# Two places of a block turn: VectorE's order and SyncE's queue where attention hands over to token mixing

## The chip, the cores and the metric

The kernel runs on one core of one Trainium2 chip. The metric is the time of one execution on the device, in microseconds (us); the number that counts is the median of several runs. The engines are named as the profile names them: PE (TensorE, matmuls), DVE (VectorE), ACT (ScalarE), POOL (GpSimd) and SP (SyncE, which here only issues transfers).

## The reference

Two stages follow each other. The first is attention restricted to clusters, for 4 batches, 8 heads, 768 tokens and 64 channels a head: each query and key is assigned to the nearest of 16 centroids, and a query sees only the keys of its own cluster. The second takes the result as `x` (4 x 768 x 512) and mixes tokens:

```python
theta = x @ w_theta
cos_t, sin_t = (np.cos(theta), np.sin(theta))
zr = x * cos_t
zi = x * sin_t
yr = np.einsum('ts,bsd->btd', w_tok_r, zr)
yi = np.einsum('ts,bsd->btd', w_tok_i, zi)
y = yr + yi
u = x + y
return (u + np.maximum(u @ w_ch, 0.0)).astype(np.float32)
```

`w_theta` is drawn large enough that the angle `theta` goes over many periods, so it is wrapped to one period before the sine.

## The kernel before, in words

Attention works through 16 pairs of heads, each in 12 units (two halves of the queries by six tiles of keys). Per unit TensorE makes the row maxima ahead of time and the scores (L374), ScalarE the exponentials (L437), GpSimd the sums of the exponentials (L448), and TensorE the weighted values (L509). What has to happen beside the units (assigning clusters, loading and splitting weights, normalising) is cut into pieces, and tables of unit numbers say at which unit each piece is recorded (`stages`, `at_unit`). `in_order` then ties the instructions of each engine to the order in which they were recorded, as far as the units go; behind that, in the mixing stage, a scheduler sets the order on each engine.

The normalised output of a pair goes to DRAM (`xT_d`, L533), with channels on partitions. The reciprocal of the row sums takes four small transfers on SyncE's queue: the sums out (`sd<-se`, L489), back in another layout (`sq<-sd`, L492), after the reciprocal on VectorE (L494) out again (`sd<-sq`, L495), and in, broadcast (`rb<-sd`, L499). VectorE or GpSimd multiplies by `rb` (L530).

Mixing goes through the 24 token tiles (4 batches of 6 tiles of 128 tokens). For each tile:

- `rotation_parts`: `x` is split in a high and a low part (`xh` on ScalarE, L581; `xl` on VectorE, L583).
- `rotation_turn`: `x` is needed a second time with tokens on partitions. Four transfers bring it from DRAM in blocks of 32 x 32 (`xb`, L596, in `load_blocks`), and one instruction on VectorE turns the blocks (`xn<-xb`, L601). `xb` has one buffer, so the blocks of the next tile are loaded when this turn has been done; `rotation_turn` issues these loads itself.
- `rotation_angle`: twelve matmuls make the angle in PSUM (`tp`, L608).
- `rotation_reduce`: VectorE wraps it to one period (`kk`, L613; `r`, L614 and L615) and ScalarE takes the absolute value (`ab`, L617).
- `rotate`: sine and cosine on ScalarE (L823), the products with `xn` on VectorE (L825), high and low parts on ScalarE (L828) and GpSimd (L830).

Then `mix` multiplies by the token weights (L876), and after the sixth tile `channel` does the last product (L899). The angle of a tile is recorded two tiles ahead of its mixing (`AHEAD`).

The change lies where the stages meet. Tile 0 is rotated while attention still runs: `first_rotation` is a generator in five pieces, recorded at units `NUT - 10 + (0, 3.5, 4, 6, 7)`. Each `yield` ends a piece:

```python
FIRST = (0, 3.5, 4, 6, 7)
stages([NUT - 10 + k for k in FIRST], first_rotation())
```

All later tiles go through `theta`, in the mixing stage; the scheduler is free to set their instructions between those of the last units. Tile 1's angle lies in the PSUM bank that tile 0's had. Beside this the last of the weight chunks is prepared: VectorE's L137 to L146 make a chunk, SyncE writes it out (`wd5i<-w`, L156). In the mixing stage SyncE reads such chunks back (`kept`, L789).

Of the kernel before, what the change touches and what calls it, by code (L numbers as in the profile page):

```python
# [41 lines left out]
def kernel(  # L42
# [153 lines left out]
    def m_tile(name):  # L196
        return ps0.tile([P, 2, 512], F32, tag="m", name=name)
# [352 lines left out]
    def first_rotation():  # L550

        xs = ma[0].tile([P, NCT, P], F32, tag="ab", name="xs")
        nc.sync.dma_start(out=xs, in_=xT_d[0][:, :, 0:P])
        yield
        load_blocks(0)
        xh, xl, xn, kk, r = rotation_tiles(0, "0_0")
        rotation_parts(xs, xh, xl)
        yield
        tp = m_tile("tp0_0")[:, 0]
        rotation_turn(0, xn)  # L560
        yield
        rotation_angle(xh, xl, tp)
        yield
        ab = rotation_reduce(0, "0_0", tp, kk, r)
        first.update(r=r, ab=ab, xn=xn)

    first = {}

    def rotation_tiles(n, name):
        pool = ma[n % 2]  # L570
        xh = pool.tile([P, NCT, P], F32R, tag="xh", name=f"xh{name}")
        xl = pool.tile([P, NCT, P], F32R, tag="xl", name=f"xl{name}")
        xn = pool.tile([P, DM], F32, tag="xn", name=f"xn{name}")
        kk = ma[0].tile([P, DM], I32, tag="kk", name=f"kk{name}")
        return xh, xl, xn, kk, pool.tile([P, DM], F32, tag="r", name=f"r{name}")

    def behind(x):
        return tc.issue_after(x.ins) if x is not None else nullcontext()

    def rotation_parts(xs, xh, xl, after=None):  # L580
        nc.scalar.copy(out=xh, in_=xs)  # L581
        with behind(after):
            nc.vector.tensor_tensor(out=xl, in0=xs, in1=f(xh), op=ALU.subtract)  # L583
# [3 lines left out]
    def load_blocks(n):  # L587
        if n == B * NT:
            return
        b, t = divmod(n, NT)  # L590
        xb = blocks[n] = ma[0].tile([P, DM], F32, tag="xb", name=f"xb{n}")


        for a in range(P // 32):
            src = xT_d[b][:, :, t * P + 32 * a:t * P + 32 * a + 32]
            nc.sync.dma_start(  # L596
                out=xb[32 * a:32 * a + 32].rearrange("c (n m r) -> c n m r", n=NP, m=P // 32),
                in_=src.rearrange("(m c) n r -> c n m r", c=32))

    def rotation_turn(n, xn):  # L600
        nc.vector.transpose(out=xn, in_=blocks.pop(n))  # L601
        load_blocks(n + 1)

    def rotation_angle(xh, xl, tp):
        n = 0
        for xx, k in ((xh, 0), (xh, 1), (xl, 0)):
            for c in range(NCT):
                nc.tensor.matmul(tp, lhsT=xx[:, c, :], rhs=w_th[c][k], start=(n == 0), stop=(n == 3 * NCT - 1))  # L608
                n += 1

    def rotation_reduce(n, name, tp, kk, r):

        nc.vector.tensor_scalar_mul(kk, tp, INV_2PI)  # L613
        nc.vector.scalar_tensor_tensor(out=r, in0=kk, scalar=-C1, in1=tp, op0=ALU.mult, op1=ALU.add)  # L614
        nc.vector.scalar_tensor_tensor(out=r, in0=kk, scalar=-C2, in1=r, op0=ALU.mult, op1=ALU.add)  # L615
        ab = ma[n % 2].tile([P, DM], F32, tag="ab", name=f"ab{name}")
        nc.scalar.activation(out=ab, in_=r, func=AF.Abs)  # L617
        return ab
# [76 lines left out]
    for x, gen in enumerate(early_weights()):  # L695
        stages(W_FIRST if x == 0 else [W_EVERY * (x - 1) + k for k in W_UNITS], gen)

    stages([NUT - 10 + k for k in FIRST], first_rotation())


# [52 lines left out]
    def mbank(name):  # L753
        return pm.tile([P, 512], F32, tag="bank", name=name)
# [49 lines left out]
    def theta(b, t):  # L804
        n, name = b * NT + t, f"{b}_{t}"
        xs = xts[b][:, :, t * P:(t + 1) * P]
        xh, xl, xn, kk, r = rotation_tiles(n, name)

        late = n == AHEAD
        rotation_parts(xs, xh, xl, last_out[0] if late else None)  # L810
        rotation_turn(n, xn)
        tp = mbank(f"tp{name}")
        with behind(last_rows[0] if late else None):
            rotation_angle(xh, xl, tp)
        ab = rotation_reduce(n, name, tp, kk, r)
        rotate(b, t, r, ab, xn)

    def rotate(b, t, r, ab, xn):
        z = []
        for nm_, tr, sc_, bi_ in (("c", ab, -1.0, halfpi), ("s", r, 1.0, 0.0)):  # L820

            with tc.issue_after(before_sin[0].ins):
                nc.scalar.activation(out=tr, in_=tr, func=AF.Sin, scale=sc_, bias=bi_)  # L823
            with tc.issue_after(before_mul[0].ins):
                nc.vector.tensor_tensor(out=tr, in0=tr, in1=xn, op=ALU.mult)  # L825
            zh = mz.tile([P, DM], F32R, tag="zh" + nm_, name=f"zh{nm_}{b}_{t}")
            zl = mz.tile([P, DM], F32R, tag="zl" + nm_, name=f"zl{nm_}{b}_{t}")
            split = nc.scalar.copy(out=zh, in_=tr)  # L828
            with tc.issue_after(last_acc[0].ins):
                nc.gpsimd.tensor_tensor(out=zl, in0=tr, in1=zh.bitcast(F32), op=ALU.subtract)  # L830
            z.append((zh, zl))
        if (b, t) == (0, 0):

            before_sin[0], before_mul[0] = split, last_sum[0]
        zs[b, t] = z
# [95 lines left out]
    for n in range(1, AHEAD):  # L931
        theta(*order[n])
    late_weights = late()
    for n, (b, t) in enumerate(order):
        if n + AHEAD < len(order):
            nb, nt = order[n + AHEAD]
            if nt == 0:
                load_x(nb)
            theta(nb, nt)
        if b == 0:  # L940
            next(late_weights, None)
        if b < B - 1 or t < NT - TAIL:
            mix(b, t)
            if t == NT - 1:
                channel(b)
# [61 lines left out]
```

## Time and profile before

| what | us |
|---|---|
| median of 3 runs | 795.83 |
| lowest and highest | 795.07 and 797.3 |
| the profiled execution's own time | 797.01 |
| its span, first to last instruction | 795.2 |
| TensorE busy | 774.7 (97%) |
| VectorE busy | 573.3 (72%) |
| GpSimd busy | 488.4 (61%) |
| ScalarE busy | 386.9 (49%) |
| mean granted TensorE clock | 0.991 |

Times in the views are counted from the start of the span. A row of the timeline gives start, duration, engine, line, operation, what it writes and reads, and in brackets how long the engine had stood idle ahead of it and what ended that. `SPq` is SyncE's queue: such a row is the issue of a transfer, not the transfer. A row of the windows gives the window, its length, the busy time of PE, PEld (weight loads), DVE, ACT and POOL with the number of instructions, the granted clock, the share of the transfer engines' time, and GB/s.

### The profile page before, as it was taken

To read this page: it belongs to the slowest core of one execution; us is meant where nothing else is said; L and a number is where in the kernel's file an instruction comes from. 1 tells how busy PE (TensorE), PEld (TensorE's weight loads), DVE (VectorE), ACT (ScalarE), POOL (GpSimd) and SP (SyncE) were. 2 spreads that over 40 slices of the span, in tenths; PEclk is the share of its full clock that TensorE was granted. 3 is DMA by queue.
4 is the path that set the end of the run, shared out by engine and by line. 5 is a ranking of instruction groups with operands and counts; after the bars stand their busy time and mean duration, and the time that the engine had idled before them with its cause. 6 is when DMAs were issued, how large, how long until landed. Compare 5 with 4: busy or idle time off the path is not lost.

```text
span 795.2 us, 14306 instructions
## 1 busy us (share of the span) xinstructions
PE 774.7 (97%) x5538; PEld 574.3 (72%) x5538; DVE 573.3 (72%) x688; ACT 386.9 (49%) x777; POOL 488.4 (61%) x284
## 2 busy tenths in 40 slices
PE   7999999999999999999999599999999999999998
PEld 5665656565665666666665378899888988899998
DVE  5889999999999999999889368954435343634322
ACT  3466666666767676666655335451324123403310
POOL 3479888999999999888988141571125122332131
PEclk9999999999999999999999899999999999999999
DMA  3233314342443234433352267024111411030001
GB/s 120 61 96 97 110 55 148 124 115 73 143 132 112 85 127 152 131 108 125 123 187 69 68 177 237 17 41 166 20 27 28 158 28 27 14 93 14 1 21 61
DMA packets 81584, 73.45 MB, mean 92 GB/s; under 512 B 59588, under 2 KB 65324, under 8 KB 81132
## 3 DMA queue, kind: packets, MB, share of 16 engines
q1 hardware_dynamic: 81228, 72.10, 30.5%
q8 instruction: 44, 0.72, 0.4%
q10 hardware_dynamic: 288, 0.43, 0.1%
q14 instruction: 24, 0.20, 0.1%
HBM read 57.08 MB, written 15.32 MB: 91 GB/s over the span
## 4 chain that ended last, share of the span: by engine, by line
PE 92%; DVE 5%; DMA 1%; SPq 1%; issue 1%; ACT 1%; DVEq 0%; ACTq 0%
PE y L876 26%; PE sc L374 25%; PE av L509 16%; PE tp L608 8%; PE cy L899 5%; PE m L374 3%; PE cp L899 3%; PE sm L476 2%; PE lg L263 1%; PE y L899 1%; DVE nm L396 1%; PE lt L275 1%; PE mt L404 1%; DVE acc L452 1%; SPq L596 1%
## 5 line engine op out<-in xcount | busy, mean ns | idle before, releaser
L437 ACT ACTIVATE at<-sc 128x384 f32<-128x384 f32 x384 | 173.6, 494 | 96.7 <-PE m L374 57.7
L396 DVE TENSOR_REDUCE nm<-m 128x1 f32<-128x768 f32 x192 | 179.7, 945 | 19.6 <-PE m L374 16.6
L448 POOL TENSOR_TENSOR acc<-at,at 128x768 f32<-128x768 f32 x64 | 130.4, 2038 | 40.0 <-ACT at L437 40.0
L374 PE MATMUL m<-hk,hq 64*128 64x384 f32 x384 | 147.2, 388 | 0.9 <-DVE nm L396 0.8
L509 PE MATMUL av<-at,vt 128*64 128x384 f32 x768 | 145.7, 499 | 1.4 <-ACT at L437 1.1
L448 POOL TENSOR_TENSOR acc<-acc,at 128x768 f32<-128x768 f32 x64 | 131.7, 2059 | 10.1 <-ACT at L437 8.0
L830 POOL TENSOR_TENSOR zlc<-ab,zhc 128x512 fp32r<-128x512 f32 x24 | 32.1, 1336 | 172.1 <-ACT zhc L828 172.1
L374 PE MATMUL m<-mk,mq 64*128 64x384 f32 x384 | 127.7, 336 | 0.6 <-DVE mk L303 0.6
L374 PE MATMUL sc<-hq,hk 64*128 64x384 f32 x384 | 117.0, 389 | 0.5 <-ACT at L437 0.5
L374 PEld LDWEIGHTS sc<-hq,hk 64*128 64x128 f32 x384 | 55.8, 183 | 61.9 <-issue 27.8
L374 PE MATMUL sc<-lq,hk 64*128 64x384 f32 x384 | 97.6, 335 | 0.0
L374 PE MATMUL sc<-mq,mk 64*128 64x384 f32 x384 | 97.4, 334 | 0.0
L374 PE MATMUL sc<-hq,lk 64*128 64x384 f32 x384 | 97.2, 333 | 0.0
L509 PEld LDWEIGHTS av<-at,vt 128*64 128x64 f32 x768 | 46.7, 136 | 60.5 <-issue 53.6
L613 DVE TENSOR_SCALAR kk<-tp 128x512 int32<-128x512 f32 x24 | 16.4, 683 | 79.4 <-PE tp L608 79.4
L374 PEld LDWEIGHTS m<-hk,hq 64*128 64x128 f32 x384 | 70.6, 185 | 3.5 <-DVE nm L396 2.7
L374 PEld LDWEIGHTS m<-mk,mq 64*128 64x128 f32 x384 | 71.3, 187 | 1.0 <-ACT hq L356 1.0
L452 DVE TENSOR_TENSOR acc<-acc,acc 128x768 f32<-128x768 f32 x30 | 70.7, 2357 | 0.0
L581 ACT CAST xh<-xT 128x512 fp32r<-128x512 f32 x23 | 14.3, 622 | 99.8 <-PE tp L608 99.8
L890 POOL TENSOR_TENSOR ul<-xT,uh 128x384 fp32r<-128x384 f32 (+1 forms) x36 | 33.5, 955 | 35.5 <-ACT uh L889 34.9
L374 PEld LDWEIGHTS sc<-lq,hk 64*128 64x128 f32 x384 | 54.9, 185 | 0.0
L374 PEld LDWEIGHTS sc<-mq,mk 64*128 64x128 f32 x384 | 54.9, 184 | 0.0
(160 smaller groups left out, 1713.3 us busy)
## 6 DMA issues: line engine op xcount, KB each, us to landing
rawq<-in_qT_dram SPq DMA_DIRECT2D x16, 384.0 KB
vt<-in_v_dram SPq DMA_DIRECT2D x16, 384.0 KB
rb<-sd SPq DMA_DIRECT2D x32, 192.0 KB
xT_d<-xt SPq DMA_DIRECT2D x16, 384.0 KB
xb<-xT_d SPq DMA_DIRECT2D x96, 64.0 KB
rawk<-in_kT_dram SPq DMA_DIRECT2D x15, 384.0 KB
w<-in_wrT_dram SPq DMA_DIRECT2D x6, 768.0 KB
w<-in_wiT_dram SPq DMA_DIRECT2D x6, 768.0 KB
```

Source lines behind the costliest of these rows:

```text
L374: nc.tensor.matmul(out, lhsT=stat[r, cols], rhs=mov[r, over], start=start, stop=stop)
L396: nc.vector.tensor_reduce(out=s["nm", a][:, j, i // 2:i // 2 + 1], in_=s["m", j][:, :, 0:HS], op=ALU.max, axis=AX.XY, negate=True)
L437: last_exp[0] = nc.scalar.activation(out=s["at", a, i][:, j], in_=s["sc", j], func=AF.Exp, scale=SCALE)
L448: last_acc[0] = nc.gpsimd.tensor_tensor(out=s["acc", a, x], in0=prev, in1=at, op=ALU.add)
L452: nc.vector.tensor_tensor(out=s["acc", a, 0], in0=s["acc", a, 0], in1=s["acc", a, 1], op=ALU.add)
L509: nc.tensor.matmul(s["av"][64 * j:64 * j + 64], lhsT=s["vt"][:, i, j, :], rhs=s["at", a, i][:, j], start=(i == 0), stop=(i == NT - 1))
L608: nc.tensor.matmul(tp, lhsT=xx[:, c, :], rhs=w_th[c][k], start=(n == 0), stop=(n == 3 * NCT - 1))
L613: nc.vector.tensor_scalar_mul(kk, tp, INV_2PI)
L830: nc.gpsimd.tensor_tensor(out=zl, in0=tr, in1=zh.bitcast(F32), op=ALU.subtract)
L876: nc.tensor.matmul(y_at(b, d, c0, c1), lhsT=zz[:, d * P:(d + 1) * P], rhs=ww[:, c0:c1], start=first and lead, stop=last, skip_group_check= ...
L890: nc.gpsimd.tensor_tensor(out=ul[:, d, :], in0=x, in1=uh[:, d, :].bitcast(F32), op=ALU.subtract)
L899: nc.tensor.matmul(cp, lhsT=w_c[d][k][:, e * P:(e + 1) * P], rhs=uu[:, d, :], start=(n == 0), stop=(n == 3 * NCT - 1), skip_group_check=True)
```

## The change

In `first_rotation` the load of tile 0's blocks moves into the first piece, next to the load of the tile itself. The turn of a tile's blocks, with the loads of the next tile's blocks that it issues, moves from ahead of the angle to behind its wrapping, in `first_rotation` and in `theta`.

```diff
         nc.sync.dma_start(out=xs, in_=xT_d[0][:, :, 0:P])
-        yield
         load_blocks(0)
+        yield
         xh, xl, xn, kk, r = rotation_tiles(0, "0_0")
         rotation_parts(xs, xh, xl)
         yield
         tp = m_tile("tp0_0")[:, 0]
+        yield
+        rotation_angle(xh, xl, tp)
+        yield
+        ab = rotation_reduce(0, "0_0", tp, kk, r)
         rotation_turn(0, xn)
-        yield
-        rotation_angle(xh, xl, tp)
-        yield
-        ab = rotation_reduce(0, "0_0", tp, kk, r)
         first.update(r=r, ab=ab, xn=xn)
...
         rotation_parts(xs, xh, xl, last_out[0] if late else None)
-        rotation_turn(n, xn)
         tp = mbank(f"tp{name}")
         with behind(last_rows[0] if late else None):
             rotation_angle(xh, xl, tp)
         ab = rotation_reduce(n, name, tp, kk, r)
+        rotation_turn(n, xn)
         rotate(b, t, r, ab, xn)
```

VectorE's order at the handover, before. `xn_0` and `xn_1` are the turns of tiles 0 and 1, `kk` and `r` the wrappings, `sq` the reciprocal of a pair's sums, `ab_0` tile 0's first product:

```order
L146 SCALAR_TENSOR_TENSOR w_5615<-w_5614,w_5615 128x768
L601 STREAM_TRANSPOSE xn_0_5829<-xb_5822 128x512
L601 STREAM_TRANSPOSE xn_1_6062<-xb_5846 128x512
L494 RECIPROCAL sq_5886<-sq_5886 128x12
L613 TENSOR_SCALAR kk_0_5830<-tp_0_5844 128x512
L614 SCALAR_TENSOR_TENSOR r_0_5831<-kk_0_5830,tp_0_5844 128x512
L615 SCALAR_TENSOR_TENSOR r_0_5831<-kk_0_5830,r_0_5831 128x512
L613 TENSOR_SCALAR kk_1_6063<-tp_1_6073 128x512
L583 TENSOR_TENSOR xl_3_6209<-xT_6021,xh_3_6208 128x512
L614 SCALAR_TENSOR_TENSOR r_1_6064<-kk_1_6063,tp_1_6073 128x512
L615 SCALAR_TENSOR_TENSOR r_1_6064<-kk_1_6063,r_1_6064 128x512
L825 TENSOR_TENSOR ab_0_5918<-ab_0_5918,xn_0_5829 128x512
```

The same place with the change:

```order
L146 SCALAR_TENSOR_TENSOR w_5615<-w_5614,w_5615 128x768
L494 RECIPROCAL sq_5880<-sq_5880 128x12
L613 TENSOR_SCALAR kk_0_5830<-tp_0_5844 128x512
L614 SCALAR_TENSOR_TENSOR r_0_5831<-kk_0_5830,tp_0_5844 128x512
L615 SCALAR_TENSOR_TENSOR r_0_5831<-kk_0_5830,r_0_5831 128x512
L601 STREAM_TRANSPOSE xn_0_5829<-xb_5755 128x512
L613 TENSOR_SCALAR kk_1_6063<-tp_1_6067 128x512
L583 TENSOR_TENSOR xl_3_6209<-xT_6021,xh_3_6208 128x512
L614 SCALAR_TENSOR_TENSOR r_1_6064<-kk_1_6063,tp_1_6067 128x512
L615 SCALAR_TENSOR_TENSOR r_1_6064<-kk_1_6063,r_1_6064 128x512
L601 STREAM_TRANSPOSE xn_1_6062<-xb_5915 128x512
L825 TENSOR_TENSOR ab_0_5912<-ab_0_5912,xn_0_5829 128x512
```

Each of the two turns has moved behind its own tile's L615; the turns of the 22 later tiles stand among the same neighbours as before, since the scheduler had put them there already. On TensorE, ScalarE and GpSimd no instruction changes places.

SyncE's queue at the same place, before. `xs` is tile 0, the first `xb` its blocks, the next two groups the blocks of tiles 1 and 2:

```order
L553 DMA xs<-xT_d_60 128x4x128
L533 DMA xT_d_63<-xt_5231 128x768
L596 DMA xb_5822<-xT_d_60 32x16x32 x4
L489 DMA sd_5840<-se_5793 4x384
L596 DMA xb_5846<-xT_d_60 32x16x32 x4
L156 DMA wd5i<-w_5615 128x768
L492 DMA sq_5886<-sd_5840 128x12
L596 DMA xb_6068<-xT_d_60 32x16x32 x2
L495 DMA sd_5841<-sq_5886 128x12
L596 DMA xb_6068<-xT_d_60 32x16x32 x2
L499 DMA rb_5939<-sd_5841 64x768 x2
L789 DMA kept<-wd3r 128x768
```

The same place with the change:

```order
L553 DMA xs<-xT_d_60 128x4x128
L596 DMA xb_5755<-xT_d_60 32x16x32 x4
L533 DMA xT_d_63<-xt_5231 128x768
L489 DMA sd_5840<-se_5798 4x384
L156 DMA wd5i<-w_5615 128x768
L492 DMA sq_5880<-sd_5840 128x12
L495 DMA sd_5841<-sq_5880 128x12
L596 DMA xb_5915<-xT_d_60 32x16x32 x4
L499 DMA rb_5939<-sd_5841 64x768 x2
L596 DMA xb_6086<-xT_d_60 32x16x32 x4
L789 DMA kept<-wd3r 128x768
```

Tile 0's blocks go ahead of the write of a normalised pair (L533). Tile 1's blocks go behind the write of the weight chunk (L156) and behind the reciprocal's transfers L492 and L495, tile 2's behind `rb`.

More of the change, by code (lines that the diff above doesn't have):

```diff
@@ L553, in first_rotation @@
         nc.sync.dma_start(out=xs, in_=xT_d[0][:, :, 0:P])
+        load_blocks(0)
         yield
-        load_blocks(0)
         xh, xl, xn, kk, r = rotation_tiles(0, "0_0")
@@ L559, in first_rotation @@
         tp = m_tile("tp0_0")[:, 0]
-        rotation_turn(0, xn)
         yield
@@ L564, in first_rotation @@
         ab = rotation_reduce(0, "0_0", tp, kk, r)
+        rotation_turn(0, xn)
         first.update(r=r, ab=ab, xn=xn)
```

## The prediction

> **What bounds the kernel now.** I began with the profile's page: the span, the engines' busy slices and the granted TensorE clock.
>
> ```profile
> span 795.2 us, 14306 instructions
> ...
> PE   7999999999999999999999599999999999999998
> ...
> PEclk9999999999999999999999899999999999999999
> ```
>
> Each digit is a slice of 19.9 us. TensorE is full everywhere except in the first slice and in slice 23 (437 to 457 us), where the attention stage hands over to the mixing stage; the clock dips there too. So an edit on VectorE or on SyncE's queue can shorten the kernel only where TensorE waits for it. TensorE's list of waits tells how much there is:
>
> ```profile
> PE tp L608 <- DVE r L614: 5.5, 1, 5.5
> PE idle L210 <- DVE identb L81: 2.6, 1, 2.6
> PE sm L476 <- DVE xt L522: 2.5, 1, 2.5
> ```
>
> The longest single wait of the run is one of 5.5 us, of tile 1's angle matmuls (L608), for VectorE. The chain of waits, in order of time, shows what stood behind it:
>
> ```profile
> 435.49 0.63 DVE xn L601
> ...
> 436.14 0.57 SPq L596
> ...
> 438.79 0.63 SPq L156
> ...
> 439.46 2.65 DMA sq<-sd
> ...
> 442.13 0.23 DVE sq L494
> 442.36 0.56 DVE kk L613
> ...
> 442.94 0.70 DVE r L614
> ...
> 443.77 5.36 PE tp L608 x12
> ```
>
> Read it backwards. Tile 1's twelve angle matmuls start when tile 0's PSUM bank has been read by the wrapping (L613, L614). The wrapping stands in VectorE's order behind a reciprocal (L494), which waits for a small transfer (sq). That transfer stands in SyncE's queue behind four block loads of tile 1 (L596), which wait for the turn of tile 0 (L601), since the blocks have one buffer. TensorE's and VectorE's rows in the timeline:
>
> ```profile
> 437.97 0.34 PE L374 MATMUL sc<-hq,hk 64*128 64x384 f32 x1
> 443.77 2.04 PE L608 MATMUL tp<-wth_hi,xh 128*128 128x512 f32 x4 [5.47 <-DVE r L614]
> ...
> 454.30 1.24 PE L509 MATMUL av<-at,vt 128*64 128x384 f32 x4 [1.15 <-ACT at L437]
> 458.00 1.76 PE L476 MATMUL sm<-acc,ecol 128*32 128x384 f32 x16 [2.46 <-DVE xt L522]
> ```
>
> ```profile
> 432.92 2.57 DVE L146 SCALAR_TENSOR_TENSOR w<-w,w 128x768 int32<-128x768 int32 x1
> 435.41 0.70 DVE L601 STREAM_TRANSPOSE xn<-xb 128x512 f32<-128x512 f32 x1
> 440.84 0.71 DVE L601 STREAM_TRANSPOSE xn<-xb 128x512 f32<-128x512 f32 x1 [4.73 <-DMA xb<-xT_d]
> ...
> 449.16 0.69 DVE L613 TENSOR_SCALAR kk<-tp 128x512 int32<-128x512 f32 x1 [4.81 <-PE tp L608]
> ...
> 456.69 0.69 DVE L825 TENSOR_TENSOR ab<-ab,xn 128x512 f32<-128x512 f32 x1 [3.49 <-ACT ab L823]
> ...
> 457.77 0.95 DVE L530 TENSOR_TENSOR xt<-xt,rb 128x768 f32<-128x768 f32 x1
> ...
> 461.39 0.70 DVE L601 STREAM_TRANSPOSE xn<-xb 128x512 f32<-128x512 f32 x1
> ```
>
> TensorE stops at 438.3 (437.97 + 0.34) and stands 5.47 us, while VectorE holds tile 0's wrapping behind two turns; the second of them alone waits 4.73 us for tile 1's blocks. From 458.0 on the chain is TensorE without a break:
>
> ```profile
> 459.76 6.78 PE tp L608 x23
> 466.54 8.41 PE y L876 x48
> ...
> 494.77 2.74 PE tp L608 x12
> ```
>
> Twelve angle matmuls take 2.74 us in that steady stage, but 5.36 at 443.77. The reason is in the stretches by window, whose column before the last two is the granted clock:
>
> ```profile
> 442.00:450.00 8.00, 6.23 (x21) 4.50 (x22) 2.99 (x6) 1.37 (x3) 0.00 (x0) 0.57 0.39 85
> 450.00:458.00 8.00, 4.39 (x26) 1.69 (x25) 4.47 (x6) 5.25 (x9) 3.62 (x2) 1.00 0.06 7
> 458.00:464.00 6.00, 6.00 (x29) 3.95 (x30) 5.77 (x7) 2.66 (x6) 3.02 (x2) 0.72 0.88 325
> ```
>
> A mean of 0.57 over 8 us, in a clock that is either full or half, is 2 x 0.43 x 8 = 6.9 us at half rate after the gap of 5.47. Another 2 x 0.28 x 6 = 3.4 us at half rate come after the gaps of 1.15 and 2.46.
>
> **The change, part by part.** On VectorE only the turns of tiles 0 and 1 change places; from tile 2 on the rows stand as before. Of the 24 turns, 22 can neither gain nor lose.
>
> Tile 1's turn leaves the front of the wrapping, and its wait of 4.73 us with it. By itself that would give nearly nothing: the reciprocal behind it started at 442.13, when its own transfer came, only 0.58 after the turn's end (440.84 + 0.71). What helps is the second effect, on SyncE's queue: the four block loads of tile 1 go behind the reciprocal's transfers, because they wait for a turn that now comes later. What is late next is then the write of a weight chunk (L156), which waits for L146 on VectorE, ended at 432.92 + 2.57 = 435.49. From that write's issue to the reciprocal the chain took 442.13 - 438.79 = 3.34 us. So: 435.5 + 3.34 = 438.8 for the reciprocal instead of 442.13; L613 and L614 follow as they did, and TensorE's matmuls start 443.77 - 442.13 = 1.64 later, at 440.5. Term one: -3.3 us. The gap becomes 440.5 - 438.3 = 2.2 us.
>
> The 3.34 was measured while block loads were under way, which the new order removes there. Bounds for issue to use come from an earlier transfer of the same tile, an upper bound since the reciprocal then stood behind another instruction:
>
> ```profile
> 410.36 0.38 SPq L492 DMA_DIRECT2D sq<-sd  x1
> ...
> 471.44 1.27 SPq L499 DMA_DIRECT2D rb<-sd  x2
> ```
>
> ```profile
> 413.98 0.22 DVE L494 RECIPROCAL sq<-sq 128x12 f32<-128x12 f32 x1
> ...
> 476.10 0.96 DVE L530 TENSOR_TENSOR xt<-xt,rb 128x768 f32<-128x768 f32 x1 [3.77 <-DMA rb<-sd]
> ```
>
> It took at most 3.62 us there against 2.65 in the chain, so term one is no smaller than 3.3 - 1.0 = 2.3. At the other end the gap can't shrink by more than if the transfer cost nothing, 3.3 + 2.65 = 5.9, and not even that, since L613 also needs tile 0's angle, which TensorE finished shortly ahead of 437.97. I keep 3.3, the chain's own row.
>
> Term two: the clock. If it stays full through a gap of 2.2 us, the twelve matmuls take 2.74 instead of 5.36: -2.6 us. The rows bracket this: full clock after the gap of 1.15, half after the one of 2.46, which came 2.4 us behind the other, so that TensorE was busy 4.39 of 8 us. Ahead of the new gap the page's slices up to 437 us read 9. I take the full clock, and keep the half one as a rival. The Trainium skill (TensorE: Matmul & The Clock Gate, section "HAM oscillation — how this bites in real kernels") asks for no idle gap of more than about 3.4 us; by that rule the old gap loses the clock and the new one doesn't, which makes the sum the same -5.9. The trace agrees for the gap of 5.47 but not for the one of 2.46, and by that row the sum would be -5.9 + 1.7 = -4.2.
>
> The early load of tile 0's blocks moves four issues ahead of one write of a normalised tile:
>
> ```profile
> 426.61 3.05 SPq L596 DMA_DIRECT2D xb<-xT_d  x4
> ...
> 444.82 2.87 SPq L499 DMA_DIRECT2D rb<-sd  x2
> 456.60 0.33 SPq L789 DMA_DIRECT2D kept<-wd3r  x1
> ```
>
> The write comes 3.05 us later and is read only in the last batch, hundreds of us on; the write of the sums behind both keeps its place. Cost 0; if something did wait for it, 3.05 at most. The early load brings nothing either: tile 0's turn did not wait for its blocks at 435.41, and now comes at about 441.
>
> Tile 0's turn costs 0.70 behind L615, that is from 441.0 to 441.7. Tile 1's wrapping, next on VectorE, waits for TensorE until 440.5 + 2.74 = 443.2: hidden, with 1.5 us to spare.
>
> Tile 1's turn now stands ahead of the first product (L825), and behind that wait the copy of the last attention output (L522), the matmuls of the sums (458.00) and all after. Its blocks' four loads can leave once tile 0's turn has ended: 441.7 to 444.4. Before, such loads went out from 436.14 to 438.8 and the turn took them at 440.84, 2.1 us behind the last issue's end. So they are there at 446.5. L825 will want to start at 456.69 - 5.9 = 450.8; with the turn itself 0.7 long, 3.6 us are to spare. Cost 0.
>
> The loads of rb now stand behind tile 1's blocks: issued from 444.4 to at most 447.3, against 444.82 to 447.69. At 471.44 to 472.71 they were followed by their user 3.4 us later, so they are in place by 450.7; L530 asks at 457.77 - 5.9 = 451.9. Cost 0, with 1.2 us to spare. Tile 2's blocks wait for tile 1's turn (end about 448), leave by 450.7 and land by 452.8; their turn comes at 461.39 - 5.9 = 455.5. Cost 0. The late weights' loads wait for the end of attention, which moves up with the rest: 456.60 - 5.9 = 450.7, just as tile 2's blocks are out.
>
> Sum: -3.3 - 2.6 = **-5.9 us**. Behind tile 1's angle everything hangs on its end, so it moves up as a whole, gaps of 1.15 and 2.46 included. The profiled execution took 797.01 (span 795.2 and 1.8 around it): 791.1. The median of the runs is 795.83, 1.2 less, and by it 789.9 results; the profiled run may have been slow in the clock, which I can't tell apart. I forecast the middle, **790.5**. A measurement of this kernel tells a change from none from about 0.3% on, 2.4 us, that is below 793.4 or above 798.2.
>
> **The rivals.**
>
> The clock drops in the short gap too, as after 2.46. One stretch of 3.4 us at half rate costs 1.7 us: 792.2; if it covers all of tile 1's angle, 2.6: 793.1. For it: the row of 458.00. Against it: the busy time ahead of the gap. 26%.
>
> More is gained: the sq transfer comes quicker with the queue empty, or the second stretch at half rate (3.4 us, 1.7 lost) falls differently and is gone: 790.5 - 1.7 = 788.8. For it: the three runs before lie 2.2 us apart (795.07 to 797.3), about what such a stretch is worth. 11%.
>
> The gain is half eaten: sq takes its upper bound (2.3 instead of 3.3), the gap is then 3.2 us, and the clock drops for the whole angle: 790.5 + 1.0 + 2.6 = 794.1, no change that can be told. 9%.
>
> Slower: the new wait takes the old one's place. Tile 1's turn holds VectorE for blocks that are ordered 5.6 us later than before (441.7 for 436.14), and L825, L522 and TensorE's sums stand behind it. It decides from a landing at 450.1 on, each us beyond costing one; nothing is left of the gain at 456, and at 459 the kernel is 3 us slower, 798.8. The loads would need 14.6 us after the last issue instead of 2.1. 4%.
>
> That the turns don't move at all is excluded for tiles 0 and 1 by the instruction order, and holds for the 22 others.
>
> **How the numbers follow.** Forecast 50%, rivals 26, 11, 9 and 4%. The range from 788.6 to 793.2 holds the forecast, the half clock and most of the larger gain, and leaves out some 15%. Faster: 50 + 26 + 11 = 87%; the same 9%; slower 4%.
>
> **What would show it.** In the profile after, TensorE's wait for L614 ahead of tile 1's angle should read about 2.2 us instead of 5.47, released by the same line; the reciprocal should follow L146 after 3.3 us idle, put down to sq; the twelve matmuls should take 2.7 us at clock 1.00; both turns should show no wait for xb; the gaps of 1.15 and 2.46 should still be there, 5.9 us earlier. Wrong I am if the gap is still above 4 us, if a turn waits for xb with TensorE behind it, or if TensorE waits later for something that wasn't in the list above.

## The result and the profile after

| | us |
|---|---|
| before, median of 7 runs (lowest, highest) | 796.01 (795.07, 797.3) |
| with the change, median of 7 runs (lowest, highest) | 790.05 (788.62, 792.87) |
| ratio, with its 95% interval | 0.993 (0.991 to 0.9949) |
| span of the profiled execution, before and after | 795.2 and 791.1 |

By the medians the change saves 6.0 us. (Of one experiment below, the early load alone, two of ten executions, the profiled one among them, took over 1000 us at a granted clock of 0.66 to 0.68, so only the times of the other eight are used.) The first view is TensorE's list of waits; the 5.5 us for L614 have become 1.4:

```profile
PE idle L210 <- DVE identb L81: 2.6, 1, 2.6
PE sm L476 <- DVE xt L522: 2.5, 1, 2.5
...
PE tp L608 <- DVE r L614: 1.4, 1, 1.4
```

The chain of waits shows what ends last now, up to tile 0's wrapping. SyncE writes the weight chunk as soon as L146 is done, sq follows it at once, and the reciprocal waits for nothing but sq:

```profile
434.33 2.52 DVE w L146
...
436.87 0.32 SPq L156
...
437.28 2.06 DMA sq<-sd
...
439.37 0.23 DVE sq L494
...
440.17 0.70 DVE r L614
```

Behind L615 this view goes on through tile 0's turn, the loads of tile 1's blocks and `rb`, which lands as one of ScalarE's exponentials starts (449.02). No time is lost there: ScalarE is not idle ahead of it, and its last two exponentials start 0.37 us apart (448.65 and 449.02), as they did before (453.77 and 454.14).

VectorE's rows in the timeline, over the same place as before:

```profile
434.25 2.58 DVE L146 SCALAR_TENSOR_TENSOR w<-w,w 128x768 int32<-128x768 int32 x1
439.37 0.23 DVE L494 RECIPROCAL sq<-sq 128x12 f32<-128x12 f32 x1 [2.53 <-DMA sq<-sd]
439.51 0.63 DVE L613 TENSOR_SCALAR kk<-tp 128x512 int32<-128x512 f32 x1
...
441.50 0.70 DVE L601 STREAM_TRANSPOSE xn<-xb 128x512 f32<-128x512 f32 x1
444.03 0.69 DVE L613 TENSOR_SCALAR kk<-tp 128x512 int32<-128x512 f32 x1 [1.82 <-PE tp L608]
...
448.00 0.70 DVE L601 STREAM_TRANSPOSE xn<-xb 128x512 f32<-128x512 f32 x1
451.57 0.69 DVE L825 TENSOR_TENSOR ab<-ab,xn 128x512 f32<-128x512 f32 x1 [2.87 <-ACT ab L823]
...
452.64 0.95 DVE L530 TENSOR_TENSOR xt<-xt,rb 128x768 f32<-128x768 f32 x1
...
456.26 0.70 DVE L601 STREAM_TRANSPOSE xn<-xb 128x512 f32<-128x512 f32 x1
```

None of the three turns (441.50, 448.00, 456.26) waits for its blocks, nor L530 for rb: no bracket stands behind these rows. TensorE's rows, and the stretches by window with the granted clock in the third column from the end:

```profile
441.01 1.16 PE L608 MATMUL tp<-wth_hi,xh 128*128 128x512 f32 x4 [1.40 <-DVE r L614]
...
449.18 1.24 PE L509 MATMUL av<-at,vt 128*64 128x384 f32 x4 [1.15 <-ACT at L437]
452.88 2.79 PE L476 MATMUL sm<-acc,ecol 128*32 128x384 f32 x16 [2.46 <-DVE xt L522]
...
462.23 0.50 PE L876 MATMUL y<-wr_hi,zhc 128*128 128x512 f32 x2
```

```profile
440.00:450.00 10.00, 7.84 (x43) 4.53 (x43) 6.78 (x9) 4.40 (x10) 2.18 (x2) 1.00 0.32 69
450.00:460.00 10.00, 7.54 (x33) 4.22 (x31) 7.25 (x9) 5.41 (x9) 4.47 (x3) 0.66 0.82 238
```

The clock stays full through the gap of 1.40 us. It still drops behind the one of 2.46.

The spans differ by 4.1 us and the medians by 6.0. The profiled execution after is the slowest of its seven (792.87), and it reached the end of L146 at 436.83 instead of 435.49, 1.3 us late. Two windows over the kernel's first slices, before and then after, show one difference ahead of the change's place:

```profile
20.00:36.00 16.00, 14.59 (x108) 10.29 (x107) 13.26 (x18) 5.57 (x13) 5.10 (x3) 0.89 0.25 73
```

```profile
20.00:36.00 16.00, 14.55 (x98) 10.21 (x97) 11.78 (x17) 4.09 (x10) 3.62 (x3) 0.79 0.23 72
```

In the profiled execution after, the clock was at half for twice as long there (2 x 0.21 x 16 = 6.7 us against 3.5), where nothing was changed. That this makes the 1.3 us is not shown: the profiles of the experiments below all read 0.79 in this window (the early load alone left out), and they reach L146's end anywhere from 435.2 to 437.1; that of the change measured once more, whose clock was also at 0.91 over the 20 us before, reached it at 435.4. So profiles are compared here from the end of L146 on, the last instruction at the handover that the change leaves alone:

| us after the end of L146 | before | after | gained by then |
|---|---|---|---|
| wrapping of tile 0 starts (first L613) | 6.79 | 2.68 | 4.1 |
| wrapping of tile 1 starts (second L613) | 13.67 | 7.20 | 6.5 |
| last sums start (L476) | 22.51 | 16.05 | 6.5 |

Each number is a row's start less that of L146's end (435.49 and 434.25 + 2.58 = 436.83). The gain is whole when tile 1's wrapping starts.

### The profile page after: what moved, and what is told of

Same layout as the page of the kernel before. It is cut to its first block, busy times and chain, and to the rows that moved or that the text cites. A ratio compares the mean times of both kernels' runs of the same rounds, so it can differ in the third digit from the quotient of the medians.

```text
span 791.1 us, 14306 instructions
## 1 busy us (share of the span) xinstructions
PE 774.3 (98%) x5538; PEld 572.9 (72%) x5538; DVE 572.6 (72%) x688; ACT 386.5 (49%) x777; POOL 488.3 (62%) x284
## 4 chain that ended last, share of the span: by engine, by line
PE 91%; DVE 5%; DMA 2%; issue 1%; SPq 1%; ACT 1%; DVEq 0%
PE y L876 26%; PE sc L374 24%; PE av L509 15%; PE tp L608 8%; PE cy L899 5%; PE m L374 4%; PE cp L899 3%; PE sm L476 2%; PE lg L263 2%; PE y L899 1%; DVE acc L452 1%; PE lt L275 1%; DVE nm L396 1%; PE mt L404 1%; DVE xl L583 1%
## 5 line engine op out<-in xcount | busy, mean ns | idle before, releaser
L448 POOL TENSOR_TENSOR acc<-acc,at 128x768 f32<-128x768 f32 x64 | 132.4, 2068 | 10.1 <-ACT at L437 8.0
L613 DVE TENSOR_SCALAR kk<-tp 128x512 int32<-128x512 f32 x24 | 16.4, 683 | 77.2 <-PE tp L608 77.2
```

The costliest lines, as they stand in the source:

```text
L448: last_acc[0] = nc.gpsimd.tensor_tensor(out=s["acc", a, x], in0=prev, in1=at, op=ALU.add)
```

## The experiments

The theory: two waits lay side by side in front of tile 0's wrapping, the turn of tile 1 (for its blocks) on VectorE and the reciprocal (for sq, behind the same blocks' loads on SyncE's queue). Both end at nearly the same time, so that one alone gives nothing; with both gone the gap also becomes short enough for the clock. Rivals: that one of the two is the whole cause, or that the early load of tile 0's blocks has a part in it. All ratios are to the kernel before on the same chip, with 95% intervals.

**The early load alone.**

```diff
         nc.sync.dma_start(out=xs, in_=xT_d[0][:, :, 0:P])
-        yield
         load_blocks(0)
+        yield
```

> Only the early load of tile 0's blocks; both turns stay in their old places. Theory of two parallel waits: nothing changes, 796 us, ratio to before 1.000, TensorE's gap ahead of tile 1's angle stays at 5.5 us, the turn of tile 1 still waits 4.7 us. Rival, the early load carries part of the gain: below 794, gap under 5 us.

Ratio 1.0001 (0.9989 to 1.0014). It gives nothing.

**The two turns alone**, that is the change without the edit above.

> Only the two turns move; tile 0's blocks are loaded in their old place. Theory: the whole gain, about 790 us, ratio 0.993, gap 1.4 to 2.2 us. Rival, the early load is needed so that tile 0's turn finds its blocks: 792 or more, with a wait of tile 0's turn for xb.

Ratio 0.9941 (0.9923 to 0.9959), tile 0's turn without a wait, and in TensorE's list:

```profile
PE tp L608 <- DVE r L614: 1.4, 1, 1.4
```

The turns carry the whole gain that can be measured; the median was 792.22 where before had 796.6. The rival's wait for xb did not come.

**Tile 1's turn alone, behind tile 0's wrapping.** `wrapped` holds tile 0's L615 (the lines that set it are left out here); tile 0's turn, and with it the loads of tile 1's blocks, stay where they were.

```diff
...
-        rotation_turn(n, xn)
+        with behind(wrapped[0] if n == 1 else None):
+            rotation_turn(n, xn)
```

> Tile 0's turn stays ahead of the reciprocal, so tile 1's block loads stay ahead of the sq transfer on SyncE's queue; only tile 1's turn, with its wait of 4.73 us, goes behind tile 0's wrapping. Theory: nothing is gained, the reciprocal still starts when sq lands, near 442.1; gap 5.4 us, 796 us, ratio 1.000. Rival, the wait in VectorE's order is the whole cause: gap about 2 us, 790 us.

Ratio 0.9997 (0.9982 to 1.0011), gap 5.19 us. VectorE's rows, then SyncE's:

```profile
434.49 2.57 DVE L146 SCALAR_TENSOR_TENSOR w<-w,w 128x768 int32<-128x768 int32 x1
...
443.41 0.23 DVE L494 RECIPROCAL sq<-sq 128x12 f32<-128x12 f32 x1 [5.72 <-DMA sq<-sd]
443.56 0.63 DVE L613 TENSOR_SCALAR kk<-tp 128x512 int32<-128x512 f32 x1
```

```profile
437.71 2.61 SPq L596 DMA_DIRECT2D xb<-xT_d  x4
440.37 0.63 SPq L156 DMA_DIRECT2D wd5i<-w  x1
441.04 0.43 SPq L492 DMA_DIRECT2D sq<-sd  x1
```

The turn's wait of 4.73 us has gone from VectorE, and in its place stands a wait of 5.72 us for sq, which goes out behind the four block loads. The longest wait ahead of the wrapping was not the cause by itself; it covered one on SyncE's queue that ended 0.58 us later.

**The sq transfer alone, ahead of tile 1's block loads.** For the pair before the last the sums are recorded earlier, and tile 1's turn keeps its place ahead of the wrapping.

```diff
-        stages([u + NU + k for k in SUMS], sums(pi))
+        stages([u + NU + k for k in (SUMS if pi != NPAIR - 2 else (4, 5, 5.9, 9, 10))], sums(pi))
```

> The sums and the sq transfer are recorded earlier, so that sq goes ahead of tile 1's block loads on SyncE's queue and the reciprocal ahead of tile 1's turn on VectorE; tile 1's turn keeps its place and its wait ahead of tile 0's wrapping. Theory: only 0.6 to 0.7 us are gained, since the wrapping then starts at the turn's end, 441.6; gap 4.8 us, 795.4 us, ratio 0.999. Rival, the queue is the whole cause: gap about 2 us, 790 us.

Ratio 0.9997 (0.9985 to 1.0009), gap 4.98 us. SyncE's rows show that sq goes out ahead of the four block loads:

```profile
432.16 0.58 SPq L492 DMA_DIRECT2D sq<-sd  x1
436.90 2.60 SPq L596 DMA_DIRECT2D xb<-xT_d  x4
```

The reciprocal comes at once, and the wrapping waits for the turn:

```profile
433.68 2.57 DVE L146 SCALAR_TENSOR_TENSOR w<-w,w 128x768 int32<-128x768 int32 x1
...
436.80 0.18 DVE L494 RECIPROCAL sq<-sq 128x12 f32<-128x12 f32 x1
441.88 0.71 DVE L601 STREAM_TRANSPOSE xn<-xb 128x512 f32<-128x512 f32 x1 [4.90 <-DMA xb<-xT_d]
442.52 0.65 DVE L613 TENSOR_SCALAR kk<-tp 128x512 int32<-128x512 f32 x1
```

The wrapping starts 6.27 us behind L146's end instead of 6.79, so 0.5 us were gained, less than the times can show. With the run above, neither wait is the cause by itself; this is what the theory asked for, and both one-cause rivals fall.

**Tile 0's turn in its old place, its loads late.** The loads of tile 1's blocks are taken out of tile 0's turn and put behind its wrapping.

```diff
         nc.vector.transpose(out=xn, in_=blocks.pop(n))
-        load_blocks(n + 1)
+        if n:
+            load_blocks(n + 1)
...
         ab = rotation_reduce(0, "0_0", tp, kk, r)
+        load_blocks(1)
```

> Tile 0's turn stays in its old place, but the loads of tile 1's blocks are issued behind tile 0's wrapping; the scheduler then sets tile 1's turn between L614 and L615 of tile 0. Theory: the sq transfer goes out as in the change, TensorE's gap ahead of tile 1's angle is again 1.4 to 2.2 us; but tile 1's turn waits about 4 us for its blocks ahead of L615, so the wrapping of tile 1 starts about 2 us later than in the change: 791 to 792 us, ratio 0.994 to 0.995. Rival, tile 0's turn has to be out of the way: gap over 4 us, 796.

Ratio 0.9979 (0.9967 to 0.9991), 795.45 us: a quarter to a third of the change's gain, and less than I expected. VectorE's rows (in this kernel the lines of `theta`'s helpers stand one or two lower: the turn is L602, the wrapping L615 to L617), then TensorE's:

```profile
433.36 2.58 DVE L146 SCALAR_TENSOR_TENSOR w<-w,w 128x768 int32<-128x768 int32 x1
...
438.62 0.63 DVE L615 TENSOR_SCALAR kk<-tp 128x512 int32<-128x512 f32 x1
...
444.68 0.71 DVE L602 STREAM_TRANSPOSE xn<-xb 128x512 f32<-128x512 f32 x1 [4.71 <-DMA xb<-xT_d]
...
446.07 0.69 DVE L615 TENSOR_SCALAR kk<-tp 128x512 int32<-128x512 f32 x1
```

```profile
440.12 1.15 PE L610 MATMUL tp<-wth_hi,xh 128*128 128x512 f32 x4 [1.40 <-DVE r L616]
...
447.58 0.44 PE L374 MATMUL sc<-hq,hk 64*128 64x384 f32 x1 [1.79 <-ACT at L437]
```

Tile 1's angle starts as early as in the change (gap 1.40), so tile 0's turn did not have to leave its place for that, and the rival falls. But the scheduler set tile 1's turn ahead of the last step of tile 0's wrapping, and there it waits 4.71 us. Tile 1's wrapping starts 10.1 us behind L146's end (446.07 - 435.94) instead of 7.2: 2.9 us are lost where I had worked out 2, and TensorE now waits for ScalarE's exponentials, which stand behind tile 0's absolute value. The last sums start 19.2 us behind L146's end, 3.3 less than before. Another 0.9 us is gone by the start of mixing (28.5 us behind L146's end, before 30.9), where the half clock lasted 10.3 us (a mean of 0.57 over the 12 us from 450) instead of 3.4. Of the 2.4 us of gain that are left at that point the medians show 1.5; that difference I can't assign. This is the rival on the slower side of the prediction, a turn that holds VectorE for late blocks, in a milder place.

**The write of the weight chunk behind sq.** This goes on from the change: what ends last there is the write's wait for L146 and then sq.

```diff
-        stages(W_FIRST if x == 0 else [W_EVERY * (x - 1) + k for k in W_UNITS], gen)
+        units = W_FIRST if x == 0 else [W_EVERY * (x - 1) + k for k in W_UNITS]
+        if x == NCT + 2 * NT - 1:
+            units = [*units[:-1], units[-1] + 1]
+        stages(units, gen)
```

> The change, with the write of the last weight chunk behind the sq transfer on SyncE's queue instead of ahead of it. Theory: what is late next in the change is that write's wait for L146; with sq ahead of it the reciprocal starts at L146's end with no wait, and L613 when tile 0's angle is done: TensorE's gap falls from 1.4 to about 0.4 us, 789 us, ratio to before 0.991 to 0.993 (against the change -1 us, which a single run may not show). Rival, the transfer itself is late: gap unchanged at 1.4 us.

```profile
433.84 2.58 DVE L146 SCALAR_TENSOR_TENSOR w<-w,w 128x768 int32<-128x768 int32 x1
436.35 0.22 DVE L494 RECIPROCAL sq<-sq 128x12 f32<-128x12 f32 x1
438.16 0.69 DVE L613 TENSOR_SCALAR kk<-tp 128x512 int32<-128x512 f32 x1 [1.60 <-PE tp L608]
```

The reciprocal waits no longer, and tile 0's wrapping starts when TensorE has made its angle. The gap is 0.52 us, and the last sums start 15.16 us behind L146's end (16.05 in the change). The ratio was 0.9908 (0.9885 to 0.993). It was then measured again, beside the change itself:

> The change with the last weight chunk's write behind the sq transfer, as before, with more rounds. Theory: the 0.9 us that the first profile showed between the end of L146 and the last sums comes back in the time: ratio 0.9915 to 0.992, 0.9 us under the change. Rival, the clock's stretches hide it: within 0.3 us of the change.

> The change itself once more, beside the two versions below on the same chip. Theory: ratio to before 0.993 again, TensorE's gap ahead of tile 1's angle 1.4 us, and a stretch at half clock behind the gap of 2.46 us. Rival, the first comparison was lucky in the clock: ratio 0.995 or above.

Here 0.9929 (0.9911 to 0.9947), beside 0.9936 (0.9914 to 0.9959) for the change, which itself had a median of 792.05 (before 796.55). The 0.9 us stand in both profiles of this version (15.16 and 15.15 us), but the medians differ by 0.7 and the intervals overlap: the times can't tell it from the change. The change's own ratio came again, and its profile shows the gap of 1.39 us and the half clock behind the one of 2.46.

**Matmuls into the gap of 2.46 us.** The second of the remaining gaps is filled, in the change, with eight matmuls whose result nobody reads.

```diff
+        if pi == NPAIR - 1:
+            fill = bank("fill")
+            for _ in range(8):
+                nc.tensor.matmul(fill, lhsT=w_th[0][0][:, 0:P], rhs=w_th[0][0], start=True, stop=True)
```

> The change, with eight matmuls into an unused PSUM bank (1.8 us of TensorE time, result not used) ahead of the matmuls of the last sums, in the gap of 2.46 us. Theory: the stretch at half clock behind that gap comes from the gap; with 0.6 us of idle time left the clock stays at 1.00 from 440 us on, the first 23 angle matmuls behind it take 5.3 us instead of 6.7, and the slowest runs go: 788.5 us, ratio 0.991, and a narrower spread. Rival, the clock drops for another reason: stretch unchanged, 790 us.

```profile
451.76 1.50 PE L480 MATMUL sm<-acc,ecol 128*32 128x384 f32 x16 [0.41 <-DVE xt L526]
```

```profile
440.00:450.00 10.00, 8.85 (x46) 5.06 (x47) 5.73 (x7) 5.10 (x9) 3.30 (x2) 1.00 0.39 79
450.00:460.00 10.00, 9.59 (x54) 6.95 (x53) 9.32 (x12) 5.58 (x10) 5.31 (x5) 1.00 0.83 239
```

The sums start when they did (16.03 us behind L146's end), and the clock is 1.00 through the whole stretch: the gap makes the drop. The time does not follow: the ratio is 0.9917 (0.9889 to 0.9945), no clear difference from the change, and the executions, from 788.94 to 793.68 us, lie no closer together. Mixing starts 2.8 us earlier (22.6 us behind L146's end instead of 25.4), but from there to the end the profile takes 331.6 us where the change takes 328.9. The scheduler made another order of the mixing stage around the eight matmuls. Its new waits in TensorE's list come to 1.7 of these 2.7 us, most of it this one; the other 1.0 us is not assigned:

```profile
PE cy L903 <- ACT uh L893: 1.3, 1, 1.3
```

**Both, the write behind sq and the filled gap.**

> The change with both: the write of the last weight chunk behind the sq transfer, and the eight unused matmuls in the gap of 2.46 us. Theory: both gains add, -1.0 and -1.5 against the change: 787.5 us, ratio to before 0.989 to 0.990. Rival, one of the two is hidden: 789.

Ratio 0.9916 (0.9894 to 0.9938), 791.02 us: the two do not add in the time. In the profile the sums start 15.2 us behind L146's end, at full clock, and the stretch from the start of mixing on is again longer, 330.5 us.

**The last sums in a bank of the scores.** TensorE's last gap waits for L522 only because the sums go to the bank that L522 empties.

```diff
-        sm = bank(f"sm{pi}") if pi < NPAIR - 1 else ps_av.tile([P, 512], F32, tag="av", name=f"sm{pi}")
+        sm = bank(f"sm{pi}")
```

> The change, with the last sums in a PSUM bank of the scores instead of the bank that the attention output leaves (L522). Theory: the wait of 2.46 us for L522 goes, the next to be late is GpSimd's last sum of exponentials: the sums start about 1.4 us earlier (14.6 instead of 16.05 us after the end of L146), gap 1.1 us, ratio 0.991. Rival, the scheduler's other order in the mixing stage or tile 2's angle gives it back: ratio 0.993 or more.

```profile
448.69 2.01 PE L476 MATMUL sm<-acc,ecol 128*32 128x384 f32 x16
...
456.19 0.50 PE L876 MATMUL y<-wr_hi,zhc 128*128 128x512 f32 x2
```

The gap has gone, the sums start 13.5 us behind L146's end, and mixing (L876) starts 6.0 us earlier than in the change's profile (456.19 against 462.23; 4.4 us of it behind L146's end). But from there to the end it takes 788.7 - 456.2 = 332.5 us, where the change takes 791.1 - 462.2 = 328.9 and before took 795.2 - 466.4 = 328.8. In all nine usable profiles without the other bank or the extra matmuls this stretch takes 328.8 to 329.0 us, so the 3.6 us come with the other order of the mixing stage. TensorE's list has 2.0 us of new waits there; the rest is not assigned. The ratio is 0.9941 (0.9918 to 0.9964): the rival.

**Both, the write behind sq and the other bank.**

> The change with both, the write behind sq and the last sums in a bank of the scores. Theory: 0.9 and 1.4 us add, the sums start 13.7 us after the end of L146, ratio 0.990, about 787.8 where before is 796. Rival: no better than either alone.

Ratio 0.9945 (0.9925 to 0.9965), 791.86 us, again no better than the change, though its profiled execution has the shortest span of all that were profiled, 787.2. I found no version that is clearly faster than the change; what was won at the handover was not seen in the medians.

## Why the prediction was right

**What bounds.** Right: the chain behind the 5.47 us was the one read backwards, and it goes through SyncE's queue. That the turn's own wait, by itself, would "give nearly nothing" was a reading of 0.58 us between two rows, and the run with tile 1's turn alone bears it out. One small misreading: the page's last slice reads 8 for TensorE, too, and not only the first and slice 23 are below 9; TensorE's list has no wait there.

**Term one, -3.3 us.** The mechanism was right, the size too small: the wrapping of tile 0 starts 4.1 us earlier. I took 3.34 us from the write's issue to the reciprocal, measured while block loads were under way; with the queue empty it is 439.37 - 436.87 = 2.50 (2.51 in the run with late loads), as the prediction had allowed in its second rival. The gap is 1.40 us and not 2.2.

**Term two, -2.6 us.** Right: the clock stayed full, and tile 1's wrapping starts 4.5 us behind tile 0's (444.03 - 439.51) instead of 6.9, 2.4 us less; the twelve matmuls took 3.0 us (441.01 to 444.00) and not 2.74. The shorter gap than forecast made this safer. The 6.9 us at half rate, which the prediction put behind the gap, began inside it, at about 442.0; the sum went by the matmuls' rows and did not suffer. But the size is partly luck. In the profiles with gaps of 5.19 and 4.98 the half clock lasted only 3.4 us (0.83 over the 10 us from 440, against 0.66 before), and tile 1's wrapping started 6.0 and 6.1 us behind tile 0's. Measured from there, this term is 1.5 or 1.6 us. The Trainium skill (TensorE: Matmul & The Clock Gate, "HAM oscillation — how this bites in real kernels") sets the limit for an idle gap near 3.4 us. The runs set it lower in this place: half clock behind gaps of 5.47, 5.19 and 4.98, full behind 1.40, and half behind the 2.46 that follows 1.15. When that gap was filled to 0.41, the drop was gone. The trace decides: 2.46 us was too long here, with 1.24 us of work between it and the gap of 1.15; what 2.46 alone does at this place no run shows.

**The costs at nothing.** All held. The first product still waited for ScalarE, with 2.87 us idle behind tile 1's turn (3.6 to spare by the forecast), rb and tile 2's blocks were there, and the early load neither gave nor cost anything.

**The sum, -5.9 us.** At the last sums it is -6.5 (22.51 - 16.05), by the medians -6.0 and in the second comparison -4.5. That 790.05 came so close to 790.5 is partly luck, since misses cancel: the quicker sq gave 0.8 us more, the clock took more back. Two things the sum did not hold. The half clock behind the gap of 2.46 lasted 6.8 us instead of 3.4 in the profile after (2 x 0.34 x 10), which takes back a us: mixing starts only 5.5 us earlier, 30.9 against 25.4 us behind L146's end. And executions differ ahead of the change's place, where the profile after lost 1.3 us.

**The rivals.** The half clock in the short gap and the slow sq did not come. Of the rival with more gain, the quicker sq came, but the second stretch at half rate, which was to go, grew longer in the profile after. The slower rival's mechanism exists, as the run with late loads shows, but not where the change puts the turn.

## What to carry to other kernels

The longest wait ahead of an instruction may cover another behind it that ends at nearly the same time: look at when the next instruction's own input came. Here moving one of the two gained 0.3 or 0.5 us, which the times don't show, and moving both brought the wrapping forward by 4.1. Work that waits for a transfer belongs behind the work that doesn't, and its loads then leave the queue free for the small transfer that someone is waiting for. An idle gap of TensorE can cost something in the clock on top of its length (2.4 us behind the gap of 5.47, 1.5 behind that of 5.19), so shortening one can be worth more than the idle time it removes.

## What had not been expected of the hardware

Executions of one kernel differ by some us: the change's ran from 788.62 to 792.87 in one comparison and from 789.44 to 794.46 in the next. The clock is a part of it: in the two profiles of the version with the write behind sq, the half clock behind the gap of 2.46 lasted 3.4 us (2 x 0.13 x 13) and 6.8 (2 x 0.26 x 13), and mixing starts 23.2 and 24.7 us behind L146's end. It is not all: of the executions with the filled gap, that of 793.68 had a mean granted clock of 0.996, that of 788.94 one of 0.993. What else differs stays open. An edit worth under 1 us, like the write behind sq, is then seen in a profile from a fixed instruction on, and not in the medians.

A matmul nobody reads, put in a gap of 2.46 us, kept the clock full and left the sums where they were; the 2.8 us that it won were lost again in the order that the scheduler made of the later stage, 331.6 us long instead of 328.9.
